# A record of its own for a row of zeros, a new written order of the work, and 22 instead of 10 dummy matmuls

## The chip, the cores and the metric

The kernel runs on one core of a Trainium2 chip. A core has five engines that each take their own instructions strictly in order: TensorE (PE, matmuls), VectorE (DVE), ScalarE (ACT), GpSimd (POOL) and SyncE (SP), which here only issues transfers. Transfers (DMAs) are issued by SP and by ACT. The metric is the device time of one execution in microseconds (us), the median of several runs.

## The reference

Two parts share one layer norm. Part A is a short convolution of k (four taps), a product with v, a long convolution over the sequence done by FFT, and a product with the normalised input. Part B is a gated MLP (gelu). The result joins them.

```python
def _A_ref(q, k, v, shift_k, ssm_k, ssm_D):      # S = 2048, D = 512
    for t in range(4):
        k_shift = k_shift + k_pad[:, t:t + S, :] * shift_k[:, 3 - t][None, None, :]
    kv = k_shift * v
    y = irfft(rfft(kv, 2 * S) * rfft(ssm_k, 2 * S))[:S] + kv * ssm_D
    return q * y
def _B_ref(x, w_gate, w_up, w_down):             # 512 -> 1792 -> 512
    return (gelu(x @ w_gate) * (x @ w_up)) @ w_down
xn = layernorm(A_q)
return A_q + _A_ref(xn, k, v, ...) * silu(_B_ref(xn, w_gate, w_up, w_down))
```

All inputs and the output are bfloat16.

## The kernel before, in words

The 2048 rows are held 16 to a partition: row 16p + t lies in partition p, tile t. Four groups (q = 0 to 3) of four tiles go through the MLP. For a group, 14 units (m) of 128 hidden columns each run four matmuls with Wg and four with Wu, 512 columns wide, into two PSUM banks; ACT takes gelu of the first into GE, DVE multiplies the second by it into HT. `down(q)` then takes HT with Wd, 14 matmuls a tile, in parts of 4, 5 and 5. Units 0 and 1 of group 0 run in halves of 256 columns. Weights come in four chunks: unit 0 and 1, units 2 to 5, 6 to 9, 10 to 13.

The layer norm (`ln`) takes two tiles at a time in group 0: statistics on DVE, the power of -0.5 on GpSimd (task 74 and 78), the scaling into XN on DVE. XN of group 0 is transposed into xnT on PE, that of the later groups by a DMA on SP's queue (`xn_transpose`, L825).

The long convolution is an FFT split in two stages of matmuls. Hn (the long filter) is loaded in four blocks and transposed on PE (L857) into HTr; stage 1 multiplies by a table of sines F1 and stores to DRAM (ZH, eight stores of 512 KB on ACT's queue). Then BH is loaded back for stage 2 (L958, 16 matmuls on 32 by 32 squares), which needs a second table TF made on GpSimd. The product of short convolution and v (the "K" side) is made on DVE in four blocks, eight operations each (L935 to L943, `kshift`), goes through the same stage 1 (ZK stores, on SP) and stage 2 (BK loads), is multiplied with the filter's spectrum, and comes back through ZI and BI.

Almost everything is written as tasks, numbered in the order in which the code adds them. What sets the order on each engine is the string SEQ: a list of task numbers (a "b" behind a number takes the task's second engine). `Sched.run` walks it and gives each task the buffers and PSUM banks that a cost model (LOAD_NS, EARLY, the durations beside each task) says are free first. Then the tasks are emitted in that order, except that the memset of zeros comes first and all loads come before the rest, in their order in SEQ. So SP issues 32 loads before anything else. The waits are not planned: `Trk` adds them by records. A record (`res`) is a range of bytes; an operation that writes it waits for all readers and writers of every overlapping record.

That touches the front. The constants: POOL makes small integer tables (tasks 2, 3, 4) and identities (5, 6), and a product (7); DVE makes phases (8: f_phase; 10: m_parts; 11: m_phase, which writes PH at L691 to L693); ACT takes sines into F1 (9) and TAB (12, then the table load for gelu at L706); POOL makes TF from TAB (13). A row of zeros, ZERO, is the first 1024 bytes of the buffer AST (1 KB of the 4 KB of its first part); PH lies in bytes 1024 to 1536 of it, TAB behind that. ZERO is used twice: as both operands of dummy matmuls on PE (task 1, `warm_up`), and as the source of a 3 KB copy ("kz", task 32, one of the loads) that puts zeros in front of the first rows of k. Both name as their record the whole first part of AST, `R_AST["K"][0]`.

```python
ZERO = AST[:, 0, 0, 0, :]
PH = at("PH", [128, 4, 32], I32, ast_at + 1024)
t_zero = S.add([("DVE", 250.0)], lambda e: trk.op("DVE", lambda h: h.memset(ZERO, 0.0), w=[R_AST["K"][0]]), w=[bwarm])
load("kz", KK[0:1, 0:3, :], ZERO[0:1, :].unsqueeze(1).broadcast_to([1, 3, 512]), [R_kz], [bKK[0]], 3072, r=[R_AST["K"][0]], rb=[bwarm])
```

The first tasks on each engine, by SEQ: DVE zeros, m_parts, f_phase, m_phase, then the statistics of x; PE the dummies, Hn's first block, the tiles of XN, Hn's second block, units 0 and 1; ACT the sines, then copies of HTr.

Of the kernel before, what the change touches and what calls it, by code (L numbers as in the profile page):

```python
# [20 lines left out]
NG = 32  # L21
LN_EPS = 1e-5
TURN = 8192
N_WARM = 10
ORDER = "x00 x01 x02 x03 w0 w1 h0 h1 h2 h3 D0 w2 s0 k0 v0 x1 w3 k1 v1 d0 d1 k2 v2 k3 v3 x2 x3"
SEQ = (
# [21 lines left out]
)  # L48
NF_BANKS = 4
ISSUE = 470.0  # L50
# [239 lines left out]
class Sched:  # L290
# [7 lines left out]
    SHARE_BW = 300.0  # L298
    FIRST = {"loads": 300.0, "SP": 30500.0}
    DRAIN = 121.0  # L300
    EARLY, LATE, SHARED, WAIT = (11000.0, 1.3), (20000.0, 1.26), 46000.0, 3300.0

    def __init__(self):
        self.tasks = []
# [86 lines left out]
def build_kernel(nc, A_q, A_k, A_v, A_shift_k, A_ssm_k, A_ssm_D, B_w_gate, B_w_up, B_w_down, out):  # L391
    with ExitStack() as es0:
# [47 lines left out]
        KK = new("KK", [128, 19, DM], BF16)  # L440
# [48 lines left out]
        trk = Trk(nc, block)  # L489
        S = Sched()  # L490
# [8 lines left out]
        def bank(b):  # L499
            return PSALL[:, 512 * b.slot:512 * (b.slot + 1)]  # L500
# [4 lines left out]
        def R_bank(b):  # L505
            return [R_ps[b.slot // 2][b.slot % 2]]
# [93 lines left out]
        def mm(h, o, l, r, st, sp):  # L600
            return h.matmul(o, lhsT=l, rhs=r, start=st, stop=sp)  # L601
# [33 lines left out]
        def pool_k():  # L635
            P(lambda h: h.iota(ARR[:, 0:2, :], [[0, 2], [16, NG]], base=1, channel_multiplier=0), [R_ARR])
            P(lambda h: h.iota(ARR[:, 2:4, :].rearrange("p a (b c) -> p a b c", c=2), [[0, 2], [512, 16], [0, 2]], base=0, channel_multiplier=0), [R_ARR])
            P(lambda h: h.iota(OFF[:, 0:2, :], [[-6144, 2], [0, 32]], base=6144, channel_multiplier=0), [R_OFF])
            P(lambda h: h.iota(OFF[:, 2:4, :].rearrange("p a (b c) -> p a b c", c=2), [[-2048, 2], [0, 16], [2048, 2]], base=6144, channel_multiplier=0), [R_OFF])

        def pool_k32():
            P(lambda h: h.iota(K32[:], [[1, 128]], base=0, channel_multiplier=-1), [R_K32])

        def pool_id():
            P(lambda h: h.memset(NHALF[:], -0.5), [R_nh])
            P(lambda h: h.tensor_scalar(ident[:], K32[:], 0.0, None, ALU.is_equal), [R_id], [R_K32])

        def pool_id32():
            P(lambda h: h.tensor_scalar(ident32[:], K32[:], 0.0, None, ALU.is_equal), [R_id32], [R_K32])

        ZERO = AST[:, 0, 0, 0, :]
        bwarm = B("warm")
        t_zero = S.add([("DVE", 250.0)], lambda e: trk.op("DVE", lambda h: h.memset(ZERO, 0.0), w=[R_AST["K"][0]]), w=[bwarm])
        warm = B("pswarm", pF)

        def warm_up(e):
            for i in range(N_WARM):
                trk.op("PE", lambda h: mm(h, bank(warm), ZERO[:, 0:128], ZERO, True, True), r=[R_AST["K"][0]], w=R_bank(warm), accum=True)

        t_warm = S.add([("PE", N_WARM * 390.0)], warm_up, r=[bwarm], w=[warm])  # L660
        bcq, bck, bid32 = B("cq"), B("ck"), B("id32")
        S.add([("POOL", 370.0)], lambda e: pool_q(), w=[bcq])
        S.add([("POOL", 470.0)], lambda e: pool_k(), w=[bck])
        bk32 = B("k32")
        S.add([("POOL", 450.0)], lambda e: pool_k32(), w=[bk32])
        S.add([("POOL", 1100.0)], lambda e: pool_id(), r=[bk32], w=[bconst, bid])
        S.add([("POOL", 950.0)], lambda e: pool_id32(), r=[bk32], w=[bid32])

        SIN_SCALE = 2.0 * math.pi / TURN * (1.0 - 2e-6)

# [6 lines left out]
        def f_mul():  # L677
            for c, off in ((0, float(TURN // 4 + TURN // 2)), (1, 0.0)):
                PO(lambda h, c=c, off=off: h.tensor_scalar(C32[:, c, :], K4[:], Q32[:, 0:1], off, ALU.mult, ALU.add), [R_Q0, R_K4], [R_C32])
# [32 lines left out]

        bFP, bQ, bMQ, bMF2 = B("fp"), B("q"), B("mq"), B("mf2")
        bFM = B("fm")
        S.add([("POOL", 700.0)], lambda e: f_mul(), r=[bcq], w=[bFM])
        S.add([("DVE", 360.0)], lambda e: f_phase(), r=[bFM], w=[bFP])
        S.add([("ACT", 510.0)], lambda e: sin(F1, C32[:], [R_C32], R_F1), r=[bFP, bcq], w=[bF1])
        S.add([("DVE", 600.0)], lambda e: m_parts(), r=[bcq], w=[bQ])
        bTAB = B("tab")
        t_mq = S.add([("DVE", 680.0)], lambda e: m_phase(), r=[bQ, bck], w=[bMQ])  # L720
        t_sin = S.add([("ACT", 1600.0)], m_sin, r=[bMQ, bcq, bF1], w=[bTAB])
        t_table = S.add([("POOL", 4500.0)], m_table, r=[bTAB], w=[bMF])
        sin_tasks = [t_sin]

        x_dr = A_q[0].rearrange("(p t) d -> p t d", t=NT)
# [45 lines left out]
        def load_halo():  # L771
            for lo, hi in ((1, 113), (113, 128)):
                src = bass.AP(k_t, A_k[0].offset + (16 * lo - 3) * DM, [[16 * DM, hi - lo], [DM, 3], [1, DM]])
                R_halo[lo] = [res(f"halo{lo}_{j}", KK[lo:hi, j, :]) for j in range(3)]
                load(f"kh{lo}", KK[lo:hi, 0:3, :], src, R_halo[lo], [bKK[0]], 3072 * (hi - lo))
            load("kz", KK[0:1, 0:3, :], ZERO[0:1, :].unsqueeze(1).broadcast_to([1, 3, 512]), [R_kz], [bKK[0]], 3072, r=[R_AST["K"][0]], rb=[bwarm])

        def load_wd(i):
            load(f"wd{i}", Wd[:, 7 * i:7 * i + 7, :], wd_dr[:, 7 * i:7 * i + 7, :], [R_Wd[i]], [bWd[i]], 917504)
# [438 lines left out]
```

## Time and profile before

| | us |
|---|---|
| median of 3 runs (216.72 to 217.69) | 217.67 |
| the profiled execution | 217.29 |
| its span, first to last instruction | 215.5 |
| PE busy, share of the span | 187.6, 87% |
| DVE busy | 157.6, 73% |
| first dummy matmul on PE | 22.70 |
| first real PE work (Hn's transposes) | 26.94 |
| last load issued by SP | 34.6 |

How to read the lines: in groups, "out<-in" are tiles, then shape and count, then busy time and mean ns, then the idle time of the engine just before them and what ended it. In a timeline the first number is the start, the second the length. "SPq" is SP's queue issuing a transfer; a transfer's row ends with its size and the time from issue to landing. A wait row names who waited, for whom, the sum, the count and the longest. Slices are fortieths of the span, in tenths.

### The profile page before, as it was taken

To read this page: it belongs to the slowest core of one execution; us is meant where nothing else is said; L and a number is where in the kernel's file an instruction comes from. 1 tells how busy PE (TensorE), PEld (TensorE's weight loads), DVE (VectorE), ACT (ScalarE), POOL (GpSimd) and SP (SyncE) were. 2 spreads that over 40 slices of the span, in tenths; PEclk is the share of its full clock that TensorE was granted. 3 is DMA by queue.
4 is the path that set the end of the run, shared out by engine and by line. 5 is a ranking of instruction groups with operands and counts; after the bars stand their busy time and mean duration, and the time that the engine had idled before them with its cause. 6 is when DMAs were issued, how large, how long until landed. Compare 5 with 4: busy or idle time off the path is not lost.

```text
span 215.5 us, 3447 instructions
## 1 busy us (share of the span) xinstructions
PE 187.6 (87%) x1353; PEld 86.0 (40%) x1368; DVE 157.6 (73%) x244; ACT 119.5 (55%) x160; POOL 17.2 (8%) x29
## 2 busy tenths in 40 slices
PE   0000789999999999999999999999999999999993
PEld 0000277544444444444334343434334344444452
DVE  2000838999999988979888887788786680677984
ACT  3000098785686885787867587567658543440112
POOL 6000283600000000000102000000000000000000
PEclk9999999999999999999999999999999999999999
DMA  5999999897032689495799999596950322756255
GB/s 154 337 314 350 364 378 365 302 187 294 0 130 81 217 300 264 158 311 214 224 356 156 280 216 319 179 329 220 306 180 27 149 97 100 285 202 188 104 185 207
DMA packets 36870, 48.66 MB, mean 226 GB/s; under 512 B 10483, under 2 KB 29815, under 8 KB 36854
## 3 DMA queue, kind: packets, MB, share of 16 engines
q1 hardware_dynamic: 31350, 40.05, 61.3%
q10 hardware_dynamic: 5504, 8.39, 10.7%
q8 instruction: 11, 0.18, 0.4%
q14 instruction: 5, 0.04, 0.1%
HBM read 27.39 MB, written 14.68 MB: 195 GB/s over the span
## 4 chain that ended last, share of the span: by engine, by line
PE 85%; SPq 5%; DMA 4%; ACT 2%; issue 1%; DVE 1%
PE psall L601 79%; SPq L573 5%; PE psall L958 5%; DMA KK<-AST 4%; ACT HTr L592 1%; PE psall L857 1%; ACT L706 1%; DVE G L1105 0%; DVE G L1104 0%; ACT xnT L592 0%; ACT TAB L702 0%; ACT G L1102 0%; DVE PH L691 0%; DVE PH L692 0%; DVE PH L693 0%
## 5 line engine op out<-in xcount | busy, mean ns | idle before, releaser
L601 PE MATMUL psall<-xnT,Wg 128*128 128x512 bf16 (+1 forms) x232 | 55.0, 372 | 0.9 <-ACT xnT L592 0.9
L601 PE MATMUL psall<-xnT,Wu 128*128 128x512 bf16 (+1 forms) x232 | 55.3, 372 | 0.0
L601 PE MATMUL psall<-Wd,HT 128*128 128x512 bf16 (+1 forms) x230 | 51.9, 367 | 0.5 <-issue 0.2
L1070 DVE TENSOR_TENSOR HT<-psall,GE 128x512 bf16<-128x512 f32 x54 | 36.8, 685 | 11.7 <-PE psall L601 11.4
L1067 ACT ACTIVATE GE<-psall 128x512 bf16<-128x512 f32 x54 | 31.0, 601 | 14.3 <-PE psall L601 12.8
L601 PEld LDWEIGHTS psall<-Wd,HT 128*128 128x128 bf16 x238 | 22.8, 98 | 25.4 <-issue 1.5
L601 PEld LDWEIGHTS psall<-xnT,Wg 128*128 128x128 bf16 x232 | 21.7, 98 | 27.4 <-issue 4.2
L601 PEld LDWEIGHTS psall<-xnT,Wu 128*128 128x128 bf16 x232 | 22.0, 98 | 26.1 <-issue 1.3
L601 PE MATMUL psall<-AST 128*128 128x512 bf16 x10 | 4.4, 628 | 22.7 <-DVE PH L693 22.7
L592 ACT ACTIVATE HS<-psall 128x1024 bf16<-128x1024 f32 x15 | 14.8, 1022 | 3.5 <-PE psall L958 3.3
L592 ACT ACTIVATE BO<-psall 128x1024 bf16<-128x1024 f32 x11 | 11.0, 1022 | 8.5 <-PE psall L958 8.0
L1096 DVE SCALAR_TENSOR_TENSOR G<-G,psall 128x512 bf16<-128x512 bf16 x12 | 8.2, 684 | 8.9 <-ACT G L1094 8.9
L939 DVE TENSOR_TENSOR KTM<-KK,SKB 128x2048 bf16<-128x2048 bf16 x12 | 14.6, 1219 | 0.1
L941 DVE TENSOR_TENSOR KAC<-KAC,KTM 128x2048 bf16<-128x2048 bf16 x12 | 14.6, 1218 | 0.1
L592 ACT ACTIVATE KB<-psall 128x1024 bf16<-128x1024 f32 x11 | 10.9, 1023 | 6.0 <-PE psall L958 6.0
L691 DVE SCALAR_TENSOR_TENSOR PH<-ARR,Q,OFF 128x128 int32<-128x128 int32 x1 | 0.4, 353 | 18.3 <-DMA KK<-AST 18.3
L702 ACT ACTIVATE TAB<-PH,COLS 128x128 f32<-128x128 int32 x1 | 0.4, 401 | 23.2 <-PE psall L601 23.2
L592 ACT ACTIVATE AST<-psall 128x1024 bf16<-128x1024 f32 x11 | 11.1, 1024 | 3.4 <-PE psall L601 3.1
L809 POOL TENSOR_TENSOR mv<-mv,NHALF 128x4 f32<-128x4 f32 (+1 forms) x5 | 4.9, 986 | 97.8 <-DVE mv L808 97.8
L1094 ACT ACTIVATE G<-psall 128x512 bf16<-128x512 f32 x12 | 7.2, 599 | 8.0 <-PE psall L601 7.8
L601 PEld LDWEIGHTS psall<-AST 128*128 128x128 bf16 x10 | 1.3, 140 | 24.9 <-DVE PH L693 22.7
L1102 ACT ACTIVATE G<-psall 128x512 bf16<-128x512 f32 (+1 forms) x5 | 2.6, 512 | 15.6 <-PE psall L601 15.6
(80 smaller groups left out, 207.9 us busy)
## 6 DMA issues: line engine op xcount, KB each, us to landing
BH<-ZH SPq DMA_DIRECT2D x8, 512.0 KB, 5.8
BK<-ZK SPq DMA_DIRECT2D x8, 512.0 KB, 6.6
HW<-HS SPq DMA_DIRECT2D x16, 256.0 KB, 4.3
ZI<-BO ACTq DMA_DIRECT2D x16, 256.0 KB, 3.1
BI<-ZI SPq DMA_DIRECT2D x8, 512.0 KB, 3.7
ZK<-AST SPq DMA_DIRECT2D x6, 512.0 KB, 3.1
Hn<-in_A_ssm_k_dram SPq DMA_DIRECT2D x4, 512.0 KB, 8.0
KK<-in_A_k_dram SPq DMA_DIRECT2D x4, 512.0 KB, 11.7
```

The lines of the kernel that those rows point to most:

```text
L573: trk.dma(eng, lambda e: e.dma_start(out=out_ap, in_=in_ap), sem, r=r, w=w)
L592: return h.activation(o, i, ACTF.Copy, scale=scale)
L601: return h.matmul(o, lhsT=l, rhs=r, start=st, stop=sp)
L809: t_pw = op([("POOL", 850.0)], lambda e, hd, ts=ts, n=n: hd.tensor_tensor(mv[:, ts, 3:4], mv[:, ts, 2:3], NHALF[:, 0:n, :], ALU.pow), r=[b ...
L939: op([("DVE", dur)], lambda e, h, j=j, m=m: h.tensor_tensor(KTM[:, m.slot, :, :], kk(j), sk(j), ALU.mult), r=need + [bSKB[j], a], w=[m], r ...
L941: op([("DVE", dur)], lambda e, h, m=m: h.tensor_tensor(KAC[:, a.slot, :, :], KAC[:, a.slot, :, :], KTM[:, m.slot, :, :], ALU.add), r=[m], ...
L958: trk.op("PE", lambda h: h.matmul(ps(s, i)[b, :], lhsT=wt(col)[a, :], rhs=data(col)[a, :], start=n < 16, stop=n >= len(todo) - 16, tile_po ...
L1067: op([("ACT", act(512))], lambda e, h: h.activation(GE[:, g.slot, :], bank(pg), ACTF.Gelu_apprx_tanh), r=[pg], w=[g], rr=lambda: R_bank(pg ...
L1070: op([("DVE", dve(512, 1))], lambda e, h: h.tensor_tensor(HT[:, q % 2, m, :], bank(pu), GE[:, g.slot, :], ALU.mult), r=[pu, g], w=[bHT[q][m]],
L1094: op([("ACT", act(n))], lambda e, h, g=g, pc=pc: h.activation(g, pc(), ACTF.Tanh, scale=0.5), r=[p], w=[bt], rr=lambda p=p: R_bank(p), ww= ...
L1096: op([("DVE", dve(512, 1))], lambda e, h, g=g, pc=pc: h.scalar_tensor_tensor(out=g, in0=g, scalar=1.0, in1=pc(), op0=ALU.add, op1=ALU.mult ...
L1102: op([("ACT", act(n))], lambda e, h, g=g, pc=pc: h.activation(g, pc(), ACTF.Silu), r=[p], w=[bt], rr=lambda p=p: R_bank(p), ww=rg, after=z ...
```

## The change

Three things. First, ZERO gets a record of its own, `R_zero`, used by the memset, the dummies and the copy into KK. Second, SEQ is another list, for the whole kernel. Third, N_WARM is 22 instead of 10. Beside them some constants of the planner's cost model change (EARLY, and the assumed durations of tasks 1, 3 to 7, 10 to 13); they emit nothing.

```diff
-N_WARM = 10
+N_WARM = 22
 SEQ = (
-    "2 0 10 3 7 15 4 8 11 1 14 67 65 16 17 69 66 5 9 68 73 22 6 71 70 23 18 74 72 12 19 48 49 77 35 24 20 78 76 30 25 83 21 26 31 75 50 51 82 52 79 "
+    "14 2 4 0 5 6 10 15 17 16 65 66 67 68 69 73 71 70 1 3 7 72 8 22 74 77 78 76 75 82 48 83 80 79 86 11 87 19 18 9 85 49 84 354 353 361 20 51b 89b "
...
-    EARLY, LATE, SHARED, WAIT = (11000.0, 1.3), (20000.0, 1.26), 46000.0, 3300.0
+    EARLY, LATE, SHARED, WAIT = (13000.0, 1.5), (20000.0, 1.26), 46000.0, 3300.0
...
         ZERO = AST[:, 0, 0, 0, :]
+        R_zero = res("ZERO", ZERO)
         bwarm = B("warm")
-        t_zero = S.add([("DVE", 250.0)], lambda e: trk.op("DVE", lambda h: h.memset(ZERO, 0.0), w=[R_AST["K"][0]]), w=[bwarm])
+        t_zero = S.add([("DVE", 250.0)], lambda e: trk.op("DVE", lambda h: h.memset(ZERO, 0.0), w=[R_zero]), w=[bwarm])
...
-                trk.op("PE", lambda h: mm(h, bank(warm), ZERO[:, 0:128], ZERO, True, True), r=[R_AST["K"][0]], w=R_bank(warm), accum=True)
+                trk.op("PE", lambda h: mm(h, bank(warm), ZERO[:, 0:128], ZERO, True, True), r=[R_zero], w=R_bank(warm), accum=True)
...
-        t_table = S.add([("POOL", 4500.0)], m_table, r=[bTAB], w=[bMF])
+        t_table = S.add([("POOL", 6200.0)], m_table, r=[bTAB], w=[bMF])
...
-            load("kz", KK[0:1, 0:3, :], ZERO[0:1, :].unsqueeze(1).broadcast_to([1, 3, 512]), [R_kz], [bKK[0]], 3072, r=[R_AST["K"][0]], rb=[bwarm])
+            load("kz", KK[0:1, 0:3, :], ZERO[0:1, :].unsqueeze(1).broadcast_to([1, 3, 512]), [R_kz], [bKK[0]], 3072, r=[R_zero], rb=[bwarm])
```

What the new SEQ says, engine by engine, as far as the prediction speaks of it:

- Loads (SP): before, the four tiles of x, Hn 0, Hn 1, Wg and Wu of units 0 and 1, group 1 of x, Hn 2, Wg of units 2 to 5, the halo of k, Hn 3, Wu of 2 to 5, ... After, the tiles of x, Hn 0, Wu and Wg of 0 and 1, Wg of 2 to 5, group 1 of x, Hn 1, the halo, Hn 3, Wu of 2 to 5, Hn 2, the taps, k's first block, the zeros, Wg of 6 to 9, k's second, Wu of 6 to 9, Wg and Wu of 10 to 13, v and k 2, both halves of Wd, v 0, v 3, v 1, and k's fourth block last.
- POOL: the identities (4, 5, 6) come ahead of the constants of PH (3) and the product (7).
- DVE: zeros, m_parts, then the whole layer norm of group 0 with f_phase inside it, then m_phase.
- ACT: two copies of xnT, then the sines.
- PE: the 22 dummies, XN's first tile, Hn 0, the other tiles, units 0 and 1, then units 2 to 5 with the other blocks of Hn between. Stage 1 of H begins with HTr's second half.
- SP behind the loads: xnT of group 1, then ZK stores, X and BH in a new mix. From stage 2 on, the order on PE is in the main that of before, with the work ahead of a task changed by some us of matmuls.

More of the change, by code (lines that the diff above doesn't have):

```diff
@@ L657, in warm_up @@
             for i in range(N_WARM):
-                trk.op("PE", lambda h: mm(h, bank(warm), ZERO[:, 0:128], ZERO, True, True), r=[R_AST["K"][0]], w=R_bank(warm), accum=True)
-        t_warm = S.add([("PE", N_WARM * 390.0)], warm_up, r=[bwarm], w=[warm])
+                trk.op("PE", lambda h: mm(h, bank(warm), ZERO[:, 0:128], ZERO, True, True), r=[R_zero], w=R_bank(warm), accum=True)
+        t_warm = S.add([("PE", 10 * 390.0 + (N_WARM - 10) * 220.0)], warm_up, r=[bwarm], w=[warm])
         bcq, bck, bid32 = B("cq"), B("ck"), B("id32")
         S.add([("POOL", 370.0)], lambda e: pool_q(), w=[bcq])
-        S.add([("POOL", 470.0)], lambda e: pool_k(), w=[bck])
+        S.add([("POOL", 1080.0)], lambda e: pool_k(), w=[bck])
         bk32 = B("k32")
-        S.add([("POOL", 450.0)], lambda e: pool_k32(), w=[bk32])
-        S.add([("POOL", 1100.0)], lambda e: pool_id(), r=[bk32], w=[bconst, bid])
-        S.add([("POOL", 950.0)], lambda e: pool_id32(), r=[bk32], w=[bid32])
+        S.add([("POOL", 260.0)], lambda e: pool_k32(), w=[bk32])
+        S.add([("POOL", 700.0)], lambda e: pool_id(), r=[bk32], w=[bconst, bid])
+        S.add([("POOL", 560.0)], lambda e: pool_id32(), r=[bk32], w=[bid32])
         SIN_SCALE = 2.0 * math.pi / TURN * (1.0 - 2e-6)
@@ L714, in build_kernel @@
         bFM = B("fm")
-        S.add([("POOL", 700.0)], lambda e: f_mul(), r=[bcq], w=[bFM])
+        S.add([("POOL", 850.0)], lambda e: f_mul(), r=[bcq], w=[bFM])
         S.add([("DVE", 360.0)], lambda e: f_phase(), r=[bFM], w=[bFP])
         S.add([("ACT", 510.0)], lambda e: sin(F1, C32[:], [R_C32], R_F1), r=[bFP, bcq], w=[bF1])
-        S.add([("DVE", 600.0)], lambda e: m_parts(), r=[bcq], w=[bQ])
+        S.add([("DVE", 800.0)], lambda e: m_parts(), r=[bcq], w=[bQ])
         bTAB = B("tab")
-        t_mq = S.add([("DVE", 680.0)], lambda e: m_phase(), r=[bQ, bck], w=[bMQ])
-        t_sin = S.add([("ACT", 1600.0)], m_sin, r=[bMQ, bcq, bF1], w=[bTAB])
-        t_table = S.add([("POOL", 4500.0)], m_table, r=[bTAB], w=[bMF])
+        t_mq = S.add([("DVE", 900.0)], lambda e: m_phase(), r=[bQ, bck], w=[bMQ])
+        t_sin = S.add([("ACT", 1900.0)], m_sin, r=[bMQ, bcq, bF1], w=[bTAB])
+        t_table = S.add([("POOL", 6200.0)], m_table, r=[bTAB], w=[bMF])
         sin_tasks = [t_sin]
```

40 rows, old and new, of the table SEQ are left out of this document.

## The prediction

> **What bounds the kernel now.** I read the page's shares, the slices, the chain that ended last, the waits and the timeline of the front, then the transfers. Shares and slices first:
>
> ```profile
> span 215.5 us, 3447 instructions
> PE 187.6 (87%) x1353; PEld 86.0 (40%) x1368; DVE 157.6 (73%) x244; ACT 119.5 (55%) x160; POOL 17.2 (8%) x29
> PE   0000789999999999999999999999999999999993
> DMA  5999999897032689495799999596950322756255
> ```
>
> TensorE (PE) is full from the fifth slice on and empty in the first four; the transfers are full in exactly those. Two windows of the busy times size it (columns: stretch, length, busy PE, PEld, DVE, ACT, POOL, clock, DMA share, GB/s):
>
> ```profile
> 26.94:43.20 16.26, 15.28 (x111) 10.93 (x112) 11.70 (x27) 13.82 (x20) 9.80 (x8) 1.00 1.03 347
> 43.20:97.14 53.94, 53.68 (x245) 24.45 (x250) 50.07 (x55) 40.04 (x52) 0.00 (x0) 1.00 0.63 194
> 97.14:211.66 114.52, 113.92 (x986) 48.92 (x994) 88.69 (x139) 63.09 (x84) 2.39 (x2) 1.00 0.68 208
> ```
>
> Once PE has begun its real work at 26.94 it idles 0.98 + 0.26 + 0.60 = 1.8 us in 185. So the end is the start of that work plus a fixed 185 us plus a tail. The waits and the timeline say why it starts so late:
>
> ```profile
> DVE PH L691 <- DMA KK<-AST: 18.3, 1, 18.3
> PE psall L601 <- DVE PH L693: 22.7, 1, 22.7
> 0.84 0.27 DVE L653 MEMSET AST<- 128x256 uint32 x1 [0.84 <-PEq L1203]
> 12.19 0.81 SPq L573 DMA_DIRECT2D KK<-AST  x1
> 21.74 0.35 DVE L691 SCALAR_TENSOR_TENSOR PH<-ARR,Q,OFF 128x128 int32<-128x128 int32 x1 [18.26 <-DMA KK<-AST]
> 22.56 1.87 DVE L800 BATCH_NORM_STATS2 stats<-X 128x6 f32<-128x512 bf16 x3
> 22.70 4.45 PE L601 MATMUL psall<-AST 128*128 128x512 bf16 x10 [22.70 <-DVE PH L693]
> 26.94 1.41 PE L857 MATMUL psall<-ident,Hn 128*128 128x128 f32 x8
> ```
>
> The zeros are set at 1.1. The small copy of zeros into KK is issued behind 18 loads and lands at 21.7. PH lies in the same record as the zeros, so writing PH waits for that copy; DVE takes its work in order, so the layer norm of the first rows stands behind PH; and the dummy matmuls read the same record, so they wait for PH too. Nothing of this is data.
>
> **The change, part by part.**
>
> *The own record of zeros.* It removes both waits. PH (from byte 1024) and TAB do not touch the zeros' 1024 bytes, so the dummies wait only for the memset, and start at about 1.2. AST's first buffer still overlaps the zeros, but it is first written by stage 1 of K, long after the copy. Adds: nothing on an engine. The first real PE work then hangs on the later of two things.
>
> *Layer norm of the first rows.* Their arrival and the steps:
>
> ```profile
> 0.72 1.83 SPq L573 DMA_DIRECT2D X<-in_A_q_dram  x4
> X<-in_A_q_dram SPq DMA_DIRECT2D x1, 128.0 KB, 2.3
> 25.70 0.73 DVE L812 TENSOR_SCALAR XN<-X,mv 128x512 bf16<-128x512 bf16 x2
> 3.17 0.30 DVE L682 TENSOR_SCALAR C<-C 128x256 int32<-128x256 int32 x1 [1.34 <-POOL C L679]
> ```
>
> The first tile lands at 0.72 + 2.3 = 3.0, the last near 2.1 + 2.3 = 4.4. From the first statistics to two normalised tiles took 25.70 + 0.73 - 22.56 = 3.9 us; the new DVE order puts f_phase (0.30) between. So tiles are ready at 3.0 + 4.2 = 7.2, with some gaps 7.8. GpSimd's reordered setup (identities ahead of the constants of PH) is the same work and is over before 4.6, as now.
>
> *22 dummies in place of 10.* Ten took 4.45, or 0.43 each; steady matmuls cost 0.22:
>
> ```profile
> 43.19 10.74 PE psall L601 x49
> ```
>
> So the added twelve cost 2.6 us at the steady rate and 5.1 at the slow one; all 22 end at 1.2 + 4.3 + 2.6 = 8.1, or at 1.2 + 9.4 = 10.6. The ten show no change of rate, and the granted clock in the rows reads 1.00 throughout, but the real work after 4.45 us of them soon runs at 0.22. I take 8.1, the row nearest in time to the change of rate. The cover is layer norm until 7.8; the uncovered 0.3 is in the sum. (The Trainium skill, TensorE: Matmul & The Clock Gate, section on the HAM clock gate, states that about 3.4 us of sustained activity doubles the rate; the ten rows at 0.43 do not show the switch within 4.3 us, and the page's own spread of ±0.5 us covers that. By the page's figure the dummies would end near 7.7, an estimate, and layer norm would set the start at 7.8.)
>
> *PE start: 26.94 to 8.1, a gain of 18.8 us*, between 19.1 (layer norm alone) and 16.3 (all dummies slow).
>
> *The new order: does the data arrive?* Issue time plus landing in the trace gives arrival against loads issued so far (MiB summed over the list):
>
> ```profile
> 2.59 0.91 SPq L573 DMA_DIRECT2D Hn<-in_A_ssm_k_dram  x2
> Hn<-in_A_ssm_k_dram SPq DMA_DIRECT2D x1, 512.0 KB, 5.7
> X<-in_A_q_dram SPq DMA_DIRECT2D x1, 512.0 KB, 8.6
> Hn<-in_A_ssm_k_dram SPq DMA_DIRECT2D x1, 512.0 KB, 11.1
> V<-in_A_v_dram SPq DMA_DIRECT2D x1, 512.0 KB, 10.5
> 25.38 4.03 SPq L573 DMA_DIRECT2D Wd<-in_B_w_down_dram  x2
> Wd<-in_B_w_down_dram SPq DMA_DIRECT2D x1, 896.0 KB, 11.5
> ```
>
> Issued at 2.59, 4.57, 8.89, 22.45 and 25.38 (five rows of the timeline; the first and last are shown), these give 1.0 MiB at 8.3, 2.5 at 13.2, 4.33 at 20.0, 8.87 at 33.0, 10.25 at 36.9. The new list of loads puts the weights of the first units ahead of Hn's second block and Hn's third behind its fourth. PE's need is 8.1 plus the work ahead of it in the new list (0.22 a 512-column matmul, 0.39 four transposes of XN, 0.52 four of Hn). Need against arrival: second Hn block 16.4 / 15.1; fourth 18.8 / 18.1; Wu of units 2 to 5 20.2 / 20.0; third Hn 21.9 / 21.4; Wg of 6 to 9 27.5 / 25.8; Wg of 10 to 13 34.0 / 30.1; Wd's halves 42.4 / 36.9 and 45.9 / 39.6. Every load is in time, four of them by less than 1 us.
>
> But now the spectrum's first stage runs while loads still run. Four of the eight ZH stores (512 KB each, issued by ACT) come, by the PE work ahead of them, at about 26 to 34. Before, they started only after the loads:
>
> ```profile
> 44.66 0.35 ACTq L573 DMA_DIRECT2D ZH<-XN  x1
> 16.20:21.60 5.40, 0.00 (x0) 0.00 (x0) 0.00 (x0) 0.00 (x0) 0.00 (x0) 1.00 1.05 348
> ```
>
> No row shows both at once. If the stores cost the loads nothing, no wait; if they take their full 2.1 MB at 348 GB/s, later loads land 6.0 us later: Wg of 10 to 13 at 33 to 36 (0 to 2 us of wait), Wd at 42.9 and 45.6 (just in time). I take 1.5, nearer the full price, since the DMA share is already 1.05. (The Trainium skill, DMA: Bandwidth & Descriptors, section Issuing engines are not separate DMA queues, says that transfers of SP and ACT interleave on the same engines; that speaks against the change and gives the 6 us, the other reading 0.)
>
> *The transposes of xn by DMA, and the middle.* The rows of group 1 (xnT) are transposed by a DMA on SP's queue behind all loads:
>
> ```profile
> 41.34 4.65 SPq L825 DMA_TRANSPOSE xnT<-XN  x1
> xnT<-XN SPq DMA_TRANSPOSE x1, 8.4
> 34.08 0.91 SPq L573 DMA_DIRECT2D V<-in_A_v_dram  x2
> ```
>
> SP is free of loads at 35.0, so xnT is there at 43.4, with the stores' 6 us at 49.4; PE wants it at 8.1 + 41.7 = 49.8. I take 0.5, between 0 and 3. Later, the K chain has no slack already:
>
> ```profile
> 102.67 0.92 SPq L573 DMA_DIRECT2D BK<-ZK  x2
> BK<-ZK SPq DMA_DIRECT2D x1, 512.0 KB, 7.0
> 109.80 0.44 PE L958 MATMUL psall<-BK,TF 32*32 32x512 bf16 x16
> 43.86 1.20 DVE L935 TENSOR_TENSOR KAC<-KK,SKB 128x2048 bf16<-128x2048 bf16 x1
> L935 DVE TENSOR_TENSOR KAC<-KK,SKB x4: 1203/1220/1222, 43.9 to 74.9; 128x2048 bf16<-128x2048 bf16 x4
> KK<-in_A_k_dram SPq DMA_DIRECT2D x1, 512.0 KB, 12.9
> SPq L171 <- DMA ZH<-XN: 20.1, 1, 20.1
> L601 PE MATMUL psall<-Wd,HT x230: 272/379/390, 62.0 to 211.9; 128*128 128x512 bf16 x101, 128*128 128x256 bf16 x14
> ```
>
> BK lands at 109.7 and is used at 109.8. In the new PE list 47 matmuls stand between the last K stage 1 and that use, 46 before, so if everything ahead moves as PE does, no wait comes. On SP, the first load of BH, which today stands behind xnT and holds the queue 20.1 us for the ZH stores, comes after two ZK stores and one load of X; the stores behind it are held less, and I count nothing for it. DVE can move: its first product of K ran at 43.9 though K's block had landed at 24.5 (11.58 + 12.9), because DVE had begun late. New, K's block lands near the same time and PE's start no longer holds DVE, so up to 18 us are there, about PE's own gain. Unshown is how much of this the middle returns: between 0 (as before, no waits) and 6 us (SP's transposes and BH, BK, BI each some tenths to 2 us late, the size of today's just-in-time margins). I take 2.0.
>
> *Other edits.* The planner's constants and costs change only the written plan's times, no instruction. PH now stands on DVE behind the layer norm and ACT's first copies of xnT stand ahead of the sines, so behind PH wait the sine of TAB, the table load for gelu, the first gelu and the GpSimd table. PH ends near 10 (7.8, two more tiles, three short steps), the sine and the load near 12; PE then has four short units in banks and free banks left, so the cost is 0, and 1 to 2 us if gelu came after 14. TF is wanted first by BH's matmuls, 60 us later.
>
> *The sum*, against the profiled execution, 217.29 (span 215.5 and 1.8 around it; 0.2% below the median of 217.67): 217.29 - 18.8 (PE start) + 1.5 (stores against loads) + 0.5 (xnT) + 2.0 (middle) = **202.5**. The ends: -19.1 and nothing back, 198.2; -16.3 with 2, 3 and 6 back, 212.0.
>
> **The rivals.**
> - *Transfers hand back much of it.* PE starts at 8 but the loads and the stores beside them are late by more than the 6 us, and SP's queue passes this on to xnT and BK. For: the transfers were full already, four needs have under 1 us of margin. Against: margins of 4 to 6 us at Wg of 10 to 13 and at Wd. With the waits at their upper bounds (2 + 3 + 6) and a late dummy end: 206 to 212.
> - *The K chain stays in its place.* If it were held by the end of the loads, BK would be used at 109.8 as now. PE comes there at 8.1 + 85.1 = 93.2 and would wait 16.6; 217.29 - 18.8 + 16.6 = 215.1, and with the stores' 1.5 it is 216.6, no change. Against: the 19 us between K's landing and its first use.
> - *The waits stay.* If another record ties the dummies or PH to the copy of zeros, PE starts at 22.7 in a plan written for 1.2: 217 or a little more. Against: the 1024 bytes of zeros meet no other buffer that is written early.
> - *Slower.* The fourth block of K, last in the new list of loads, comes after DVE's present time for it, 74.9 (the last start in the L935 row). From there to BK's use are 34.9 us, so each us of lateness is a us of time: at 80 it is 222. It decides from 74.9. All loads (13.3 MiB) and the ZH stores (4 MiB) by then need 18.1 MB in 72 us, 252 GB/s; the rows have 347 while loads run. So the transfers would have to lose a quarter of their rate.
>
> **How the numbers follow.** The forecast, 198 to 206: 0.71. Transfers hand back much, 206 to 212: 0.19. K chain in place, about 216.6: 0.04. Waits stay, about 217: 0.03. Slower, about 222: 0.03. The range 198 to 210 leaves out the last three (0.10) and the second's upper end (0.06), and so holds about 0.84; the forecast's own is 198 to 206. A measurement here tells 0.5% (about 1.1 us) from no change. Faster takes the first two and half of the third: 0.92. Same, half of the third and half of the fourth: 0.04. Slower: 0.04.
>
> **What would show it.** Right: no DVE wait for the copy of zeros; statistics of X from about 3 and PE's dummies from about 1.2, the last ten or so at 0.22; transposes of XN on PE at 8 to 9; the first down matmul on Wd at 42 to 45 (62.0 now); first use of BK at 93 to 98; PE idle after its real start 4 to 8 us, as against 1.8. Dummies all at 0.43, or ending past 9, would show the upper price. Waits of PE for xnT or for Wg, Wu, Wd by DMA between 20 and 55 show the first rival; BK's use at 109 the second; PE's first matmul at 20 or later the third; L935's last start past 75 the fourth. The prediction is wrong if PE's idle time after 8 us is above 12 us, or if PE's steady matmul leaves 0.22.

## The result and the profile after

| | before | after |
|---|---|---|
| median of four runs each, us | 217.31 (216.72 to 217.69) | 200.62 (199.68 to 203.58) |
| ratio, 95% interval | | 0.922 [0.917, 0.927] |
| profiled execution, us | 217.29 | 200.59 |
| its span, us | 215.5 | 198.8 |
| start of the first real PE work, us | 26.94 | 8.22 |
| PE's idle time from there to its last matmul, us | 1.84 | 4.29 |

The change takes 16.7 us off; 202.5 was forecast, in a range of 198 to 210. Some executions of a kernel are disturbed, longer and at a lower granted clock: the medians count them, the ratios do not, and three profiles caught one (the first of the changed kernel, 203.58 us, that of the doubled stores and that of the record alone with task 451 moved), so the rows of the changed kernel are from a second profile of it where nothing else is said.

The shares of the engines and the slices of the changed kernel, to be held against those of before:

```profile
span 198.8 us, 3465 instructions
PE 190.0 (96%) x1365; PEld 87.1 (44%) x1380; DVE 160.8 (81%) x248; ACT 115.9 (58%) x157; POOL 16.6 (8%) x29
PE   7999799999599999999999999999999999999993
DMA  5999999999547997399999995862554314966146
```

Four slices stood empty before. Now PE is busy from the first slice on (with the dummies), and after them only the fifth (7), the eleventh (5) and the last are not near full. PE's waits in the whole span (who waited for whom, sum, count, longest):

```profile
PE psall L601 <- DMA xnT<-XN: 1.9, 1, 1.9
PE psall L601 <- DVE Q L686: 1.2, 1, 1.2
PE psall L601 <- DVE HTr L595: 1.1, 1, 1.1
PE psall L601 <- issue: 0.5, 3, 0.2
PE psall L601 <- ACT GE L1059: 0.2, 1, 0.2
```

The 22.7 us that PE waited for PH are gone. The 1.2 us for Q are the wait for the memset ahead of the dummies. Two rows are new in the stretch of real work: 1.9 us for the transpose of xn by DMA, and 1.1 us for DVE's copy of HTr. Their places, in PE's timeline (start, length, and the idle time before it):

```profile
1.17 7.21 PE L601 MATMUL psall<-AST 128*128 128x512 bf16 x22 [1.17 <-DVE Q L686]
8.22 0.39 PE L834 MATMUL psall<-ident,XN 128*128 128x128 bf16 x4
...
23.01 0.61 PE L601 MATMUL psall<-HTr,F 128*128 128x512 bf16 x2 [1.08 <-DVE HTr L595]
...
42.47 1.03 PE L601 MATMUL psall<-Wd,HT 128*128 128x512 bf16 x4
...
51.91 1.89 PE L601 MATMUL psall<-xnT,Wg 128*128 128x512 bf16 x8 [1.94 <-DMA xnT<-XN]
```

The windows of busy times give the balance (columns as in the prediction): from the start of real work to the end of the last matmul, 195.50, PE is busy for 182.99 of 187.28 us. Before it was 182.88 of 184.72.

```profile
8.22:195.50 187.28, 182.99 (x1344) 84.37 (x1357) 154.10 (x225) 114.19 (x155) 11.59 (x10) 1.00 0.78 247
```

So the work is the same to 0.1 us, and the time is made up of the start (-18.72), the longer stretch (187.28 - 184.72 = +2.56) and a tail that is 198.8 - 195.50 = 3.30 where it was 3.84 (-0.54): together -16.70, and 217.29 - 16.70 = 200.59.

### The profile page after: what moved, and what is told of

It is laid out like the page before. It is cut to its first block, busy times and chain, and to the rows that moved or that the text cites. A ratio compares the mean times of both kernels' runs of the same rounds, so it can differ in the third digit from the quotient of the medians.

```text
span 201.8 us, 3480 instructions
## 1 busy us (share of the span) xinstructions
PE 193.1 (96%) x1380; PEld 87.5 (43%) x1380; DVE 160.9 (80%) x248; ACT 115.8 (57%) x157; POOL 16.6 (8%) x29
## 4 chain that ended last, share of the span: by engine, by line
PE 87%; DMA 7%; ACT 2%; DVE 2%; issue 0%
PE psall L601 80%; DMA xnT<-XN 7%; PE psall L959 5%; PE psall L858 1%; DVE HTr L595 1%; DVE XN L813 1%; ACT L707 1%; ACT L703 1%; DVE HT L1071 0%; ACT xnT L592 0%; DVE G L1106 0%; DVE G L1105 0%; ACT F L703 0%; PE psall L834 0%; ACT G L1103 0%
## 5 line engine op out<-in xcount | busy, mean ns | idle before, releaser
L601 PE MATMUL psall<-xnT,Wg 128*128 128x512 bf16 (+1 forms) x232 | 56.1, 378 | 3.3 <-DMA xnT<-XN 3.2
L601 PE MATMUL psall<-Wd,HT 128*128 128x512 bf16 (+1 forms) x238 | 54.1, 367 | 0.0
L592 ACT ACTIVATE BO<-psall 128x1024 bf16<-128x1024 f32 x10 | 10.0, 1024 | 13.2 <-PE psall L959 13.2
L592 ACT ACTIVATE HS<-psall 128x1024 bf16<-128x1024 f32 x13 | 12.8, 1026 | 4.9 <-PE psall L959 4.9
L592 ACT ACTIVATE AST<-psall 128x1024 bf16<-128x1024 f32 x10 | 10.1, 1025 | 7.0 <-PE psall L601 7.0
L801 DVE BATCH_NORM_STATS2 stats<-X 128x6 f32<-128x512 bf16 x16 | 10.5, 676 | 1.6 <-DMA X<-in_A_q_dram 1.6
L1022 DVE TENSOR_TENSOR HS<-KB,HS 128x1024 bf16<-128x1024 bf16 x16 | 10.9, 682 | 0.0
L1022 DVE TENSOR_TENSOR HW<-KB,HW 128x1024 bf16<-128x1024 bf16 x16 | 10.9, 682 | 0.0
L592 ACT ACTIVATE X<-psall 128x1024 bf16<-128x1024 f32 x8 | 8.2, 1022 | 4.2 <-PE psall L601 4.2
L595 DVE CAST KB<-psall 128x1024 bf16<-128x1024 f32 x6 | 7.3, 1224 | 4.1 <-PE psall L959 4.1
```

The source lines that it names most:

```text
L592: return h.activation(o, i, ACTF.Copy, scale=scale)
L595: return h.tensor_copy(o, i)
L801: t_stats[t] = op([("DVE", 670.0)], lambda e, h, t=t: h.bn_stats(stats[:, t, :], X[:, t, :]), r=[bX[q][t % 4]], w=[bst[t]], rr=[R_X[t]], w ...
L1022: return hd.tensor_tensor(o, flat(KB, kb[h]), o, ALU.mult)
```

## The experiments

My theory ahead of the first of them: the record frees the start, the order lets the data keep pace with it, neither gives the gain alone, and what is handed back lies mainly in the transpose of xn (task 451) behind the stores. The rival: the record does it all, and order and dummies add nothing. Expectations stand as they were written before each run. Ratios are against the kernel before on the same chip, with their 95% interval.

**The changed kernel again**, unedited, as the base of the others.

> The changed kernel again, unedited, for a second profile and an interval. If the 3.2 us wait of PE for the transpose of group 1 (DMA xnT<-XN) and the slow matmuls behind it belong to the kernel, they are here again, in a span of about 198 to 199. If they belong to that one execution, PE is busy through 43 to 60 us and the span is about 195 to 196. Time 199.5 to 201.

Measured: 200.14 us, ratio 0.922 [0.917, 0.928]. Its rows are those above.

**The record alone**, in the kernel before, with its old order and ten dummies.

```diff
+        R_zero = res("ZERO", ZERO)
         (memset: w=, dummies: r=, copy into KK: r=)
-        R_AST["K"][0]
+        R_zero
```

> The kernel before with the zeros' own record and nothing else: old order, 10 dummies. Theory A (the false wait is all that was slow): PE begins real work when Hn's first block lands, at 8.3, in place of 26.9, and the later needs (Wu of units 2 to 5 at 21.5, Wg of 6 to 9 at 26) are met by the old order too: 199 to 203. Theory B (the gain needs the new order as well, because the old list brings the second pair of weights too late for PE that starts at 8): waits of PE for Wg and Wu between 10 and 35 us add 4 to 8: 204 to 209.

Measured: 208.90 us, ratio 0.961 [0.956, 0.966]: 8.1 us, about half of the gain. PE's timeline and two windows of its clock:

```profile
8.10 1.94 PE L858 MATMUL psall<-ident,Hn 128*128 128x128 f32 x8 [3.13 <-DMA Hn<-in_A_ssm_k_dram]
...
59.07 1.44 PE L601 MATMUL psall<-xnT,Wg 128*128 128x512 bf16 x3 [7.87 <-DMA xnT<-XN]
```
```profile
8.10:12.00 3.90, 3.90 (x29) 3.82 (x30) 3.59 (x5) 2.45 (x3) 3.90 (x3) 0.63 1.04 354
59.10:62.00 2.90, 2.90 (x7) 0.96 (x8) 0.00 (x0) 0.17 (x1) 0.00 (x0) 0.50 0.19 71
```

PE's real work starts at 8.1 here too. What the old order lacks comes later: xnT was issued at 39.18 and landed 19.8 us after, and PE waited 7.87 us for it. Behind the two gaps PE works at a granted clock of 0.63 and 0.50 for some 3 to 4 us. Against the changed kernel the longer wait (7.87 - 1.94 = 5.9) and the slow stretches (3.90 x 0.37 + 2.90 x 0.50 = 2.9), less the 1.1 us for HTr, make 7.7 us. The two profiled executions lie 7.4 apart (207.96 and 200.59), the medians 8.8.

**The record alone, with task 451 ahead of three loads**: is that wait what the old order lacks?

```diff
-        order.sort(key=...)
+        late = [S.tasks[n] for n in (42, 43, 39)]
+        order = [t for t in order if t not in late]
+        order.sort(key=...)
+        at451 = order.index(S.tasks[451]) + 1
+        order[at451:at451] = late
```

> The kernel before with the zeros' own record, and SP's transpose of group 1 ahead of its last three loads (k 2, v 2, v 1). With the record alone PE waited 7.9 us for that transpose, and its clock was granted lower behind it. Theory A (that wait is nearly all that the old order lacks): 199 to 201. Theory B (the old order costs as much elsewhere, or the three loads, now later, hold DVE up): 204 to 208.

Measured: 203.21 us, with a wide spread (200.34 to 205.15), ratio 0.930 [0.922, 0.938]. PE's wait for xnT is gone from the profile; in its place stand 2.3 us for DVE's product of V, with DVE itself held 5.4 us by a block of k that now loads later, and 2.3 us for Hn at the start remain. So it seems that most of what the new order adds to the record is that one transfer in time. The spread does not allow a finer figure.

**The new order and the 22 dummies alone**, with the zeros back on the old record.

```diff
-        R_zero
+        R_AST["K"][0]
```

> The changed kernel with the zeros on AST's record again: new order, 22 dummies. The dummies stand ahead of PH now, so they run at 1.2 all the same, and layer norm does not stand behind PH. PH waits for the copy of zeros, which lands near 20. Behind it: sine, table load, gelu, so the first gelu is at about 22 to 24 in place of 13.6, and PE, with its banks full, waits some 8 to 10 us from about 14. Theory A: 204 to 209 (part of it taken back where PE waits for xnT today). Theory B (the order alone does it): 200 to 202. If the order is worth nothing without the record: 215 to 218.

Measured: 213.23 us, ratio 0.981 [0.975, 0.986]. One wait of DVE, one row of PE's timeline, and PE's clock in that stretch:

```profile
DVE PH L691 <- DMA KK<-AST: 13.4, 1, 13.4
```
```profile
23.92 5.30 PE L601 MATMUL psall<-xnT,Wg 128*128 128x256 bf16 x16 [11.90 <-DVE xnT L595]
```
```profile
23.92:29.20 5.28, 5.28 (x17) 2.54 (x18) 2.71 (x6) 3.34 (x8) 5.20 (x3) 0.50 1.09 361
```

The layer norm now stands ahead of PH, so PE begins its real work at 8.22 even on the old record. But PH still waits for the copy of zeros, and DVE's copy of xnT is queued behind PH: PE stops at 12 for 11.9 us and then works 5.3 us at half the clock. The dummies start at 1.17 here too, since PH comes behind them. The order alone is worth 3.8 us (under 2%, though its interval stays below 1), the record alone 8.1, both together 16.9 in this set of runs, 5.0 more than the two added: each takes away a wait that the other leaves.

**Task 451 ahead of three loads**, in the changed kernel: does the 1.94 us wait hang on the place in SP's queue? The edit is that of the run above, on v's second block (39), k's fourth (44) and v's last (45).

> The changed kernel, with the transpose of group 1 issued by SP ahead of the last three loads (v 1, v 3, k's fourth block) in place of behind them. If PE's wait for that transpose is on the path, it goes: the transpose is issued near 34 in place of 39.3 and lands at 44 to 48, before PE wants it at 50; no slow matmuls behind it: 196 to 198.5. If the three loads that now come some 6 us later hold up DVE's K blocks and with them BK, the time stays at 199.5 to 201 or rises.

Measured: 198.38 us, ratio 0.912 [0.908, 0.917]; 1.8 us better than the unedited kernel. SP's rows, first of the changed kernel, then of the edited one:

```profile
30.73 7.36 SPq L573 DMA_DIRECT2D V<-in_A_v_dram  x3
38.14 0.67 SPq L573 DMA_DIRECT2D KK<-in_A_k_dram  x1
38.85 9.55 SPq L826 DMA_TRANSPOSE xnT<-XN  x1
```
```profile
36.65 7.31 SPq L826 DMA_TRANSPOSE xnT<-XN  x1
```
```profile
50.11 1.89 PE L601 MATMUL psall<-xnT,Wg 128*128 128x512 bf16 x8
```

Issued 2.2 us earlier and landed in 10.8 instead of 12.9, the transpose is there at 47.5, and PE takes it at 50.11 without a wait. This is the best version found. A second set of runs of it gave:

> The changed kernel with the transpose of group 1 ahead of the last three loads, once more beside the others: 198.4 as in its first runs, within 0.5.

Measured: 199.05 us (198.14 to 202.13, six runs), ratio 0.916 [0.912, 0.920].

**Each early ZH store issued twice**, in the changed kernel, the second time into a tensor that nothing reads: do the stores delay the loads?

```diff
+                if x == "H" and u >= 4:
+                    dma(e, bass.AP(ZX, ...), ..., dsem(f"d_zx{u}"), [R_AST...], [])
```

> The changed kernel, in which each of the four ZH stores that run beside the loads is issued a second time, into a tensor that nothing reads: 2.1 MB more on ACT's queue between 26 and 40 us. If stores delay the loads byte for byte, SP ends its loads some 5 us later (44 in place of 38.9), the transpose of group 1 lands some 5 us later and PE's wait grows from 1.9 to about 7, with slow matmuls behind so long a gap: 205 to 208. If the loads are held by something else (their own rate, the memory), SP ends them at 39 to 40 and the time stays within 1 us of 200.

Measured: 207.84 us, ratio 0.944 [0.941, 0.948]; four runs from 204.51 to 211.06, so the mechanism is read from the profile and not the size:

```profile
43.28 9.86 SPq L827 DMA_TRANSPOSE xnT<-XN  x1
```
```profile
45.67 1.02 PE L602 MATMUL psall<-Wd,HT 128*128 128x512 bf16 x4 [2.48 <-DMA Wd<-in_B_w_down_dram]
...
59.89 3.57 PE L602 MATMUL psall<-xnT,Wg 128*128 128x512 bf16 x8 [6.72 <-DMA xnT<-XN]
```

SP gets to the transpose 4.4 us later than in the rows above (38.85). Held against the first profile of the changed kernel, it is 4.0 later (39.26 there), and PE's wait for xnT is 3.6 us longer (3.16 there). The added 2.1 MB are 6.0 us at the 348 GB/s of the prediction and 5.2 at the 403 GB/s that the changed kernel moves from 28 to 39 us, while loads and stores run together. So most of what stores move is taken from the loads, which agrees with the Trainium skill (DMA: Bandwidth & Descriptors, section Issuing engines are not separate DMA queues). In place of the prediction's 6 us for 2.1 MB these rows give 4.0 to 4.4. Smaller stores were not tried: they would leave part of ZH unwritten.

**40 dummies, and 40 dummies with task 451 early**: how much of PE's early start can be given away?

```diff
-N_WARM = 22
+N_WARM = 40
```

> The changed kernel with 40 dummies in place of 22: 18 more at 0.216, so PE's real work begins 3.9 us later, near 12.1. Theory A (the transpose of group 1 lands at its own time, set by the transfers, and PE waits 1.9 us for it): the wait swallows 1.9 of the 3.9, and the time rises by 2.0 to about 202. Theory B (PE's start alone sets the end): it rises by 3.9 to about 204.

> 40 dummies, and the transpose of group 1 ahead of the last three loads. There is no wait left for it to swallow, so a start 3.9 us later is an end 3.9 us later: 198.4 + 3.9 = 202.3, by either theory; by theory A the same time as 40 dummies without the move, by theory B 1.8 below it.

Measured: 202.07 us, ratio 0.932 [0.930, 0.934], and 202.34 us, 0.933 [0.930, 0.936]. PE's dummies and SP's transpose in the first of the two:

```profile
1.17 10.45 PE L601 MATMUL psall<-AST 128*128 128x512 bf16 x40 [1.17 <-DVE Q L686]
```
```profile
34.26 13.03 SPq L826 DMA_TRANSPOSE xnT<-XN  x1
```

Real work starts at 11.46, 3.24 us later, yet the time is only 1.9 longer: PE's wait for xnT, 1.94, is gone. It asks later, and the stores come later too, so SP is free of loads at 34.26. With the transpose early as well there is no wait left to swallow a delay, and the whole of it shows: real work starts at 11.71, 3.5 us later, and the time is 3.3 to 4.0 longer (from 199.05 and 198.38, its two sets of runs, to 202.34). Behind the front, the time follows PE's start.

**Ten dummies with task 451 early**: what do the added twelve bring?

```diff
-N_WARM = 22
+N_WARM = 10
```

> 10 dummies in place of 22, with the transpose of group 1 ahead of the last three loads (198.4 with 22). The dummies end near 5.4, normalised rows are ready at 7.6 as before. Theory A (the second dozen buys the clock: an idle stretch of 3 us before the first real work brought a granted clock of 0.63 over the next 4 us in the kernel with the record alone): the first 4 us of real work are slower by 1 to 2 us, 199 to 200.5. Theory B (the dozen is only in the way, since it ends after the rows are ready): PE starts 0.3 to 0.6 us earlier and nothing is slower, 197.8 to 198.2.

Measured: 199.63 us, ratio 0.916 [0.912, 0.921], as against 199.05 on the same chip with 22: the intervals overlap. With ten, PE starts 0.43 us sooner (7.87 against 8.30), but does its first transposes at half the rate: eight of XN take 1.06 us, against 0.61 for the same tiles in the changed kernel. The first unit's Wu comes at 10.92, against 10.19, and the later wait for HTr is 2.09 us, against 1.64.

```profile
7.87 0.61 PE L834 MATMUL psall<-ident,XN 128*128 128x128 bf16 x4 [2.25 <-DVE XN L813]
8.27 1.06 PE L858 MATMUL psall<-ident,Hn 128*128 128x128 f32 x4
9.12 1.06 PE L834 MATMUL psall<-ident,XN 128*128 128x128 bf16 x8
...
10.92 0.60 PE L601 MATMUL psall<-xnT,Wu 128*128 128x256 bf16 x4
```

The medians put the twelve dummies at about 0.6 us, which these runs do not tell from nothing; they do not carry the change.

**19 dummies, task 451 early, and Wu of unit 4 ahead of the first stage 1** (task 378 ahead of 115 in SEQ), against the wait for HTr.

```diff
-    "... 59b 115 378 116 ..."
+    "... 59b 378 115 116 ..."
```

> Three small edits on the changed kernel: the transpose of group 1 ahead of the last three loads, 19 dummies (they end near 7.6, when the first rows are ready), and the Wu matmuls of unit 4 ahead of the stage 1 task that waits 1.1 to 1.4 us for a copy of HTr on DVE. If each is on the path: 198.4 - 0.6 - 1.2 = 196.6. If DVE only hands the wait on: 197.5 to 198.4.

Measured: 199.67 us (198.31 to 200.98), ratio 0.919 [0.914, 0.923]: no gain over 199.05. PE's timeline:

```profile
18.89 1.89 PE L601 MATMUL psall<-xnT,Wu 128*128 128x512 bf16 x8
23.10 1.04 PE L601 MATMUL psall<-HTr,F 128*128 128x512 bf16 x4 [1.02 <-DVE HTr L595]
24.82 0.61 PE L601 MATMUL psall<-HTr,F 128*128 128x512 bf16 x2 [0.69 <-ACT X L592]
25.73 0.61 PE L601 MATMUL psall<-HTr,F 128*128 128x512 bf16 x2 [0.31 <-ACT XN L592]
...
28.35 1.89 PE L601 MATMUL psall<-xnT,Wg 128*128 128x512 bf16 x8
```

At 18.89 PE is 0.76 us ahead of the second set of runs of the kernel with 22 dummies and task 451 early (19.65 there); at 28.35 it is level with it (28.40). The lead goes into three small waits for DVE and ACT. Between 20 and 26 us these two set the pace, and PE's place in front of them does not matter.

## Why the prediction was right, and where it was not

*PE's start* (-18.8 forecast, -18.72 measured) was right, and by the steps given: dummies from 1.17, the first real matmul behind them at 8.22 (8.1 forecast), the layer norm ready before. The weight loads of the dummies show the change of rate:

```profile
4.99 0.15 PEld L601 LDWEIGHTS psall<-AST 128*128 128x128 bf16 x1 [0.28 <-issue]
5.42 0.15 PEld L601 LDWEIGHTS psall<-AST 128*128 128x128 bf16 x1 [0.28 <-issue]
5.84 2.05 PEld L601 LDWEIGHTS psall<-AST 128*128 128x128 bf16 x10 [0.28 <-issue]
```

They stand 0.43 us apart until 5.84, and the last ten take 2.05 us together; so ten or eleven of the added twelve ran at the steady rate, nearly as taken. The change came 4.7 us after the first dummy (1.17 to 5.87, eleven matmuls at 0.43). The prediction let the spread of ±0.5 us that it names from the Trainium skill (TensorE: Matmul & The Clock Gate, section on the HAM clock gate) cover the ten slow rows; but 3.4 and 0.5 are 3.9, short of those rows' 4.3 and of the 4.7 here. With 22 of them the start hung on the dummies, with ten on the layer norm (7.87).

*Stores against loads* (+1.5 at the weights and Wd): the mechanism held, the place did not. Wd's halves were issued at 24.8 and 25.25, and the transfers of the tile took

```profile
DMA to landing us min/median/max: 16.1/17.2/18.2
```

so they landed at 40.9 and 43.4, about 4 us later than the 36.9 and 39.6 that stood without stores, but earlier than the 42.9 and 45.6 of the full price. What the queues moved from 28 to 39 us (packets, MB, share of the DMA engines; q1 is SP's queue, q10 ACT's), before and after:

```profile
q1 hardware_dynamic: 2626, 4.15, 107.1%
```
```profile
q1 hardware_dynamic: 1593, 2.32, 57.4%
q10 hardware_dynamic: 576, 2.10, 46.7%
```

While the stores move 2.10 MB, the loads move 1.83 MB less than before. PE took Wd's first half at 42.47, 1.6 us after its landing, and waited for no weights: this term measured 0. Doubling the stores used the margin up and brought a wait for Wd.

*The transpose of xn* (+0.5, between 0 and 3) is the term that was mis-sized: 1.94. The step laid the stores' 6 us on a landing at 43.4, with SP free of loads at 35.0 and 8.4 us of transfer. Measured, SP was free at 38.85 and the transpose took 12.9 to land, so xnT came at 51.8: 8.4 us late, not 6.0, and PE wanted it at 49.97. The weak number is the 8.4. In the kernel before, SP issued the transpose 6.3 us after it was free of loads, so more than half of the last load's 11.5 us to landing was over by then. The landings, in us, from the issue and landing rows of each run:

| run | transpose issued | last load ahead of it landed | transpose landed |
|---|---|---|---|
| before | 41.34 | 46.1 | 49.7 |
| changed kernel | 38.85 | 48.5 | 51.8 |
| changed kernel, task 451 early | 36.65 | 44.2 | 47.5 |
| stores doubled | 43.28 | 53.3 | 59.8 |
| record alone | 39.18 | 51.2 | 59.0 |

The transpose lands behind the last load that SP issued ahead of it, by 3.2 to 3.7 us in the first three rows. By that it could not have come at 43.4 even without stores: in the kernel before, whose first store was issued at 44.66, the last load landed at 46.1. In the changed kernel ACT's queue moves nothing from 39 to 45 us and SP's queue 2.4 MB, so what the transpose waits for in this stretch is the backlog of loads, which the stores had delayed before. That stores also slow the transpose itself is not shown here; what makes the last two rows' 6.5 and 7.8 us is open. The early transpose shows that its place behind the loads is the cause of PE's wait: the wait went, and the time with it.

*The middle* (+2.0, between 0 and 6) measured 0. PE waited for no BK, BH or BI. DVE's first product of K ran at 25.1 instead of 43.9 and BK's first use came at 95.07 instead of 109.8:

```profile
L936 DVE TENSOR_TENSOR KAC<-KK,SKB x4: 1215/1219/1219, 25.1 to 57.7; 128x2048 bf16<-128x2048 bf16 x4
```
```profile
L959 PE MATMUL psall<-BK,TF x128: 384/385/386, 95.1 to 155.7; 32*32 32x512 bf16 x128
```

With that fell the rival in which the K chain keeps its place (109.8) and the one that ends slower: the fourth block was used at 57.7, far from the 74.9 at which it decides. The one in which the waits stay fell with PE's first matmul at 1.17.

*Not foreseen* were 1.1 us at 23.0 for HTr, where DVE had two XN scalings and an HT ahead of the copy, and 0.5 us of the tail, won.

So the three terms that were to hand back 4.0 us handed back 2.0 (2.56 less 0.54): 1.94 and 1.08 for the two waits, 0.16 for gelu, less 0.5 of tail and 0.6 of small gaps that before were larger. The likeliest case of the prediction was the right one, and its sum 1.9 us too high: 3.5 us for waits that did not come, less 2.5 for xnT and HTr that were priced too low or not at all and 0.2 for gelu, and the 1.1 of tail and small gaps. That the sum came so near is in part luck: these errors have opposite signs. The start, which makes nearly the whole gain, was not luck. The rival in which transfers hand back much, 206 to 212, was reached only with twice the stores.

## What to carry to other kernels

A record that covers more bytes than the operation uses makes waits that no data needs: where a chain shows an engine waiting for a small transfer that it never reads, ask which bytes the two share. Removing such a wait is half of the work; the other half is the order behind it, and here the queue of loads had one transfer (the transpose) that was worth moving up. Read margins at the queue that issues the transfer: stores beside loads delay the loads, and a transfer issued behind those loads landed only after them, so its time from issue to landing counts their backlog too.

## What the runs showed of the hardware that was not expected

PE's rate after a gap. The wait of PE, and the granted clock of the stretch right behind it:

| run | PE waited, us | granted clock, stretch |
|---|---|---|
| changed kernel | 1.94 | 1.00 (51.90 to 54.00) |
| record alone, task 451 early | 2.29 | 0.62 (60.06 to 64.50) |
| stores doubled | 2.48 | 1.00 (45.67 to 48.00) |
| record alone, at the front | 3.13 | 0.63 (8.10 to 12.00) |
| changed kernel, first profile | 3.16 | 0.58 (53.25 to 56.40) |
| stores doubled | 6.72 | 0.50 (59.89 to 63.40) |
| record alone | 7.87 | 0.50 (59.10 to 62.00) |
| order alone | 11.90 | 0.50 (23.92 to 29.20) |

The windows behind the first of these and the gap of 3.16:

```profile
51.90:54.00 2.10, 2.04 (x9) 0.99 (x11) 2.10 (x3) 0.60 (x1) 0.00 (x0) 1.00 0.17 68
```
```profile
53.25:56.40 3.15, 3.15 (x9) 1.20 (x10) 2.03 (x2) 0.60 (x1) 0.00 (x0) 0.58 0.00 0
```

The gaps of 1.94 and 2.48 us cost only themselves; the others cost themselves and 1.3 us (3.15 x 0.42) to 2.6 us (5.28 x 0.50) of slow matmuls behind them, a price that the prediction had for none of its waits. The length of the gap alone does not decide, since 2.29 us were followed by a fall and 2.48 us were not. Away from the front, narrow windows show when the clock falls, an estimate from their means: 3.3 us after PE stopped (gap of 2.29), 3.7 (3.16), 4.4 (6.72), 4.2 (7.87) and 4.1 (11.90). In the first two PE had been at work again for 1.0 and 0.5 us when it fell. The Trainium skill (TensorE: Matmul & The Clock Gate, section on the HAM clock gate) puts the idle time after which the rate is halved at about 3.4 us. These falls lie at it or up to 1 us above, but two gaps shorter than it paid as well, each a single one.

The granted clock reads 1.00 while the first dummies run 0.43 us apart, and again in the half-rate stretch behind ten dummies and a gap of 2.25 us (7.87 to 10.90), which is why that gap is not in the table. At the front of a kernel the matmul's own duration tells the rate, not that column.

The DMA transpose of one and the same tile took 8.4 us from issue to landing in the kernel before, 12.9 in the changed one, 16.5 with the stores doubled and 19.8 with the record alone. The table of landings above shows that the loads ahead of it make much of that: counted from the last of them, it came 3.7, 3.2, 6.5 and 7.8 us later.
